# Linear attention, then a GELU projection: steps 13 to 17 of the attention in batches instead of one by one

## The chip, the cores and the metric

The kernel runs on one core of a Trainium2 chip. The metric is the time of one execution in device microseconds. Every run gives one such time; the profile is of a single execution, taken by the hardware profiler. The engines of the core are named as the profile names them: PE (TensorE, matrix multiply; PEld is its weight load), DVE (VectorE), ACT (ScalarE), POOL (GpSimd) and SP (SyncE, which issues nearly all transfers).

## The reference

Two stages. The first is a linear attention with decay, over 4 batches, 8 heads, 768 positions and 64 channels. Written in blocks:

```python
for b in range(nb):                       # 12 blocks of 64 positions
    intra = einsum('bhic,bhjc->bhij', qb, kb) * Dmask      # Dmask: lam^(i-j) where i >= j
    intra = einsum('bhij,bhjd->bhid', intra, vb)
    inter = einsum('bhid,bhde->bhie', qb * lam_pow, kv_state)
    out[:, :, sl] = intra + inter
    kv_state = lam_block * kv_state + einsum('bhsd,bhse->bhde', kb * rev_pow, vb)
```

The second takes its output as 3072 tokens of 512 channels:

```python
h = x @ w_in                              # 512 -> 2048
g = gelu_tanh(h)
out = g @ w_out                           # 2048 -> 512, float32
```

## The kernel before

**Steps.** The attention is cut into 24 steps. A step is 256 positions of one batch and four of the eight heads, so steps 2b and 2b+1 are the two halves of the heads for "super-block" b. Batches have three super-blocks each. One step goes through these pieces, named by their functions and by the tiles they write:

- `load_step(s)` (L70): three transfers of 256 KB issued by SP: q, k and v in float32.
- `prep_qk(s)`: the cast of q with its decay on DVE (L271), the cast of k on ACT (L276), both into one tile `qk`; from step 9 on, a transposing transfer issued by SP (L280) that writes `qkT`. The pool of `qkT` has four buffers, so the transpose of step n waits until step n-4 has read its own for the last time.
- `prep_v(s)`: v with the inverse decay on POOL (L258), and then the loads of step s+3.
- `scores(n)` (L327): 16 small matmuls on 64x64 quarters of PE, into two PSUM banks S.
- `causal(n)` (L337): DVE masks the two banks into the f16 tile PT, 128x512 each.
- `products(n, s)` (L362, L376, L385): into two banks OK, the products k.v of step n (16 small matmuls, 8 where a batch ends), PT.v of the step before (16 small ones), and state.q of the step before (two or four full-size ones).
- `x_out` (L462): ACT copies the output of a step into xT, the input of the second stage.
- `update(n, 0)` and `update(n, 1)`: the state t on DVE (L478 or L481) and its two-head form u on POOL (L488). u is what the step's state.q products read.

`R(n, s)` is scores, products, masks and the first update; `U(n)` is the second update. `burst(ns, ss)` does the same for several steps at once: all scores, then all PT.v into banks O (L411), all k.v into banks K (L425), all state.q (L436), and only then the masks. A burst of two steps takes four S, two O and two K banks, which are all eight banks of PSUM.

**The second stage** runs in groups of super-blocks: group 3 is super-blocks 4 and 5 (steps 8 to 11), group 4 is 6 and 7 (steps 12 to 15), group 5 is 8 and 9. `queue_group(g)` is called when the last step of a group has its output; it appends the group's pieces to a list, `filler`, and `fill(n)` takes the next n of them. For groups 3 and 4 there are 16 pieces of four matmuls 128x512 (Hps, L529), each with a GELU on ACT (L533) that empties the bank, and then 14 products of eight matmuls 128x256 (MX, MW and MY, L606), which use a scheme of seven products for eight. That scheme needs four sums of GELU outputs, `sum_g`, on DVE (gs, L576), each in two halves; `behind(k, ...)` attaches sums to the k-th piece, so that they are put on DVE's queue after it. `sum_win` (L151) forms sums of w_in on DVE, which are first read by the pieces of group 5 (L698).

**Order.** It is written out by hand: every engine works through its instructions in the order in which the program records them, and waits at the first whose inputs or buffer are not there. Steps 8 to 17 are taken one by one, in a loop over the table FILL: `fill`, `prep(n+2)`, `fill`, `R(n, n-1)`, `fill`, `U(n)`, `fill`, and a sum of w_in. Steps 18 to 23 are taken in bursts of two.

Of the kernel before, what the change touches and what calls it, by code (L numbers as in the profile page):

```python
# [9 lines left out]
FP16 = mybir.dt.float16  # L10
AF = mybir.ActivationFunctionType
ALU = mybir.AluOpType
# [3 lines left out]
def kernel(  # L16
# [10 lines left out]
    nc = tc.nc  # L27
    pin = tc.keep_in_program_order
    P = 128
    B, H, S, D = q.shape  # L30
    SB = 256
    NSB = S // SB
    HH = H // 2
# [12 lines left out]
    a16p = ctx.enter_context(tc.tile_pool(name="a16", bufs=5))  # L46
# [11 lines left out]
    ld32 = {}  # L58
# [85 lines left out]
    def sum_win(m, j, eng):  # L144

        if not wi_sum:
            wi_sum.extend(wst.tile([P, 2, 2, DFF // 2], FP16, tag=f"w{2 + i}", name=f"ws{i}")
                          for i in range(2))
        a, op, b = I_SUMS[m]
        cs, fs = slice(0, 2), slice(512 * j, 512 * j + 512)  # L150
        pin(eng.tensor_tensor(w_in_block(m, cs, fs), w_in_block(a, cs, fs),  # L151
                              w_in_block(b, cs, fs), op))
# [17 lines left out]
    def load_ahead(s):  # L170
        if s < NSTEP:
            load_step(s)
# [40 lines left out]
    dv = const.tile([P, H, 2], FP32)  # L213
# [31 lines left out]
    def prep(s):  # L245
        prep_qk(s)
        prep_v(s)

    def wide(t):
        return t.rearrange("p j h d -> p h j d")  # L250

    def decay(t, s):
        hs = halves[s % 2]
        return t[:, hs, :].unsqueeze(3).to_broadcast([P, HH, 2, D])

    def prep_v(s):
        tv = a16p.tile([P, 2, HH, D], FP16, tag="v16", name=f"v16_{s}")
        pin(nc.gpsimd.tensor_tensor(wide(tv[:]), ld32[s][2][:], decay(dv, s), ALU.mult))  # L258
        a16[s] = a16[s] + (tv,)
        if s >= 6:  # L260
            if s + 3 == FIRST_DMA_T + 1:
                load_step(s + 3, "qk")
            else:
                load_ahead(s + 3)

    def prep_qk(s):
        q32, k32, _ = ld32[s]
        tqk = a16p.tile([P, 2, 2, HH, D], FP16, tag="qk16", name=f"qk16_{s}")
        tq, tk = tqk[:, 0], tqk[:, 1]
        q_eng = nc.gpsimd if s == 3 else nc.vector  # L270
        pin(q_eng.tensor_tensor(wide(tq), q32[:], decay(dq, s), ALU.mult))  # L271
        if s == 0:
            inverse(halves[0])
            odd(halves[1])
            inverse(halves[1])
        pin(nc.scalar.activation(out=wide(tk), in_=k32[:], func=AF.Copy))  # L276
        a16[s] = (tq, tk)
        if s >= FIRST_DMA_T:
            o = qkp.tile([P, 2, 2, 2, P], FP16, tag="qkT", name=f"qkT_{s}")
            pin(nc.sync.dma_start_transpose(out=o[:].rearrange("p a j h t -> p (a j h) t"),  # L280
                                            in_=tqk[:].rearrange("p a j h d -> p (a j h d)")))
            qkT[s] = o
            if s == FIRST_DMA_T:
                load_step(s + 1, "v")
# [107 lines left out]
    def burst(ns, ss, *mix):  # L392


        for n in ns:
            scores(n)
        O = [ps_M.tile([P, 2, 2, P], FP32, tag="M", name=f"O{c}") for c in range(2)]
        seen = set()

        def start(kind, c, hl):  # L400
            new = (kind, c, hl) not in seen
            seen.add((kind, c, hl))
            return new

        qTs = [qkT.pop(s) for s in ss]
        for i, s in enumerate(ss):
            PT, tv = PTs.pop(s), a16.pop(s)[2]
            for hp in range(2):
                for jk in range(2):
                    for c, hl in TILES:  # L410
                        pin(nc.tensor.matmul(  # L411
                            O[c][half64(hl), i, hp, :], tv[half64(c), jk, 2 * hp + hl, :],
                            PT[half64(c), hl, hp, jk, :], start=start("O", c, hl), stop=False,
                            skip_group_check=True))
        if ns:
            K = [ps_M.tile([P, 2, P], FP32, tag="M", name=f"K{c}") for c in range(2)]
        for i, n in enumerate(ns):
            _, tk, tv = a16[n]
            last = (n // 2) % NSB == NSB - 1
            for jk in range(2):  # L420
                for hp in range(2):
                    for c, hl in TILES:
                        if c == 1 and last:
                            continue
                        pin(nc.tensor.matmul(  # L425
                            K[c][half64(hl), i, hp * D : hp * D + D],
                            tk[half64(c), jk, 2 * hp + hl, :], tv[half64(c), jk, 2 * hp + hl, :],
                            start=start("K", c, hl), stop=(jk == 1), skip_group_check=True))
            Kps[n] = [t[:, i] for t in K]
        for i, s in enumerate(ss):  # L430
            for c in range(2):
                if c == 0 and (s // 2) % NSB == 0:
                    continue
                u = us.pop((s, 0) if c else (s - 2, 1))
                for hp in range(2):
                    pin(nc.tensor.matmul(O[c][:, i, hp, :], u[:, hp].rearrange("p l d -> p (l d)"),  # L436
                                         qTs[i][:, 0, :, hp, half64(c)], start=False, stop=True,
                                         skip_group_check=True))
        for n in ns:
            causal(n)  # L440
        for i, s in enumerate(ss):
            x_out(s, [t[:, i].rearrange("p h t -> p (h t)") for t in O])
        sbg = ss[-1] // 2
        g, i = group_of[sbg]
        if i == len(groups[g]) - 1:
            queue_group(g, *mix)
        for n in ns:
            update(n, 0)
# [63 lines left out]
    def queue_group(g, lead=0, per_set=0):  # L512
# [69 lines left out]
        def product(m, p, part=None):  # L582
# [42 lines left out]
            def store(T, ps=slice(0, NP), es=slice(0, 2)):  # L625
                r = row0 + T * HN
                rows = out[r : r + HN, :].rearrange("(p q) (e d) -> q p e d", q=P, e=2)
                whole = g == 3 or (g, T) == (4, 0)
                for i in [ps] if whole else [slice(i, i + 1) for i in range(ps.start, ps.stop)]:
                    pin(nc.sync.dma_start(out=rows[:, i, es], in_=out_tile(T)[:, i, es, :]))  # L630

# [180 lines left out]
        def behind(k, i0, i1, ms):  # L812

            piece = filler[at + k]

            def both():
                piece()
                sum_g(i0, i1, ms)

            filler[at + k] = both  # L820
# [21 lines left out]
        if per == 2:  # L842
            behind(5, 0, 4, (1, 2))
            behind(6, 0, 4, (4, 3))
            behind(7, 4, 8, (1,))
            behind(8, 4, 8, (2,))
            behind(9, 4, 8, (4,))
            behind(10, 4, 8, (3,))
        else:
            behind(9, 0, 4, (1, 2, 4, 3))  # L850
            w = 2 if g + 1 in SEVEN else 1
            for k, m in zip((0, 3, 7, 11) if w == 2 else (0, 1, 2, 4), (1, 2, 4, 3)):
                behind(n1 + k, 4, 8, (m,))

    def fill(n):
        for _ in range(min(n, len(filler))):
            filler.pop(0)()

    def R(n, s, ahead=None):

        if n is not None:
            scores(n)
        if ahead:
            ahead()
        products(n, s)
        if n is not None:
            causal(n)
        if s is not None and s % 2 == 1:
            g, i = group_of[s // 2]
            if i == len(groups[g]) - 1 and g > 0:  # L870
                queue_group(g)
        if n is not None:
            update(n, 0)

    def U(n):
        update(n, 1)
# [63 lines left out]
    for m in W_SUMS:  # L940
# [29 lines left out]
    prep_v(9)  # L970
    fill(2)

    FILL = {8: (0, 2, 1, 2), 9: (2, 2, 1, 2), 10: (0, 1, 1, 3), 11: (0, 2, 1, 2), 12: (0, 2, 1, 3),
            13: (0, 2, 1, 3), 14: (0, 3, 1, 3), 15: (0, 2, 1, 3), 16: (0, 2, 1, 3), 17: (0, 3, 1, 3)}
    for n, (a, b, c, d) in FILL.items():
        stage_t(n)
        fill(a)
        prep_qk(n + 2) if n == 8 else prep(n + 2)
        fill(b)
        R(n, n - 1)  # L980
        fill(c)
        U(n)
        if n == 8:
            prep_v(n + 2)
        if n == 17:
            prep_qk(20)
            fill(1)
            prep_qk(21)
            fill(1)
            prep_v(20)  # L990
            prep_v(21)
            fill(1)
        else:
            fill(d)
        if 8 < n < 17:
            sum_win((n - 7) // 2, (n - 1) % 2, nc.vector)

    burst((18, 19), (17,))
    fill(2)
    U(18)  # L1000
    U(19)
# [47 lines left out]
```

## Time and profile before

| | |
|---|---|
| median of 7 runs | 200.19 us (199.78 to 202.28) |
| the profiled execution | 199.67 us, of which the span from first to last instruction is 197.9 us |
| PE busy | 192.6 us, 97% of the span |
| DVE, ACT, POOL busy | 151.8, 123.1, 73.2 us |
| granted TensorE clock | 1.000 |
| scores of step 13 / of the burst of 18 and 19 start | 86.80 / 117.74 us |

Times inside the execution are microseconds from the start of the span. In the timeline a row is `start, duration, engine, line, operation, out<-in, tile, shape, count`, and what stands in brackets is idle time before it and what ended it. The ends of matmuls are modelled; their starts can be trusted, so the cost of a stretch of PE is read from one start to another.

### The profile page before, as it was taken

The page shows a single profiled execution, that of the slowest core. Times are in us where ns is not written, and L with a number is a line of the kernel's source. Part 1 is how long each engine was busy: PE and PEld are TensorE (multiplying, and loading weights), DVE is VectorE, ACT ScalarE, POOL GpSimd, SP SyncE. Part 2 cuts the span into 40 slices and gives each one's busy share as a digit, 9 for nine tenths or more (in the row PEclk, how much of TensorE's full clock was granted, in tenths as well). Part 3 has the DMA queues.
Part 4 walks back from the last instruction along what each step waited for, and adds up shares of the span by engine and source line. Part 5 has one row for each costly group of instructions (what it writes and reads, how often), then busy time and mean ns, then how long its engine had stood idle before and what let it go on. Part 6 is the DMA issues. An engine that isn't in the chain of part 4 may idle for free.

```text
span 197.9 us, 5938 instructions
## 1 busy us (share of the span) xinstructions
PE 192.6 (97%) x2439; PEld 140.2 (71%) x2439; DVE 151.8 (77%) x296; ACT 123.1 (62%) x251; POOL 73.2 (37%) x85
## 2 busy tenths in 40 slices
PE   8979999999999999999999999999999999999993
PEld 2556544456888888754588754578888888888882
DVE  4797623689999989949898378998778997588620
ACT  3673878466793674577735486854668836778221
POOL 6594123456457643435533465056002030002000
PEclk9999999999999999999999999999999999999999
DMA  6999999999999999999854999530211300030205
GB/s 173 291 325 387 385 386 386 297 290 303 322 265 264 220 299 228 208 318 193 226 144 111 265 230 230 145 56 0 53 45 64 107 7 0 0 108 2 106 3 212
DMA packets 61706, 37.86 MB, mean 191 GB/s; under 512 B 17520, under 2 KB 54640, under 8 KB 61680
## 3 DMA queue, kind: packets, MB, share of 16 engines
q1 hardware_dynamic: 61136, 37.23, 72.9%
q8 instruction: 19, 0.31, 0.7%
q10 hardware_dynamic: 544, 0.26, 0.5%
q14 instruction: 7, 0.06, 0.1%
HBM read 27.26 MB, written 6.29 MB: 170 GB/s over the span
## 4 chain that ended last, share of the span: by engine, by line
PE 88%; SPq 4%; DMA 4%; ACT 1%; issue 1%
PE Hps L529 24%; PE MX L606 17%; PE MY L606 9%; PE HX L698 7%; PE O2ps L544 7%; PE MW L606 4%; DMA wi<-in_moe_w_in_dram 4%; SPq L70 4%; PE HY L698 4%; PE S L327 3%; PE Hps L789 3%; PE OK L385 2%; PE HW L698 2%; PE OK L376 2%; PE Tps L298 1%; PE O L436 1%
## 5 line engine op out<-in xcount | busy, mean ns | idle before, releaser
L529 PE MATMUL Hps<-xT,w_in 128*128 128x512 f16 (+1 forms) x288 | 51.0, 332 | 0.0
L488 POOL TENSOR_TENSOR u<-t,lumask 128x256 f16<-128x256 f32 x40 | 29.5, 749 | 49.2 <-DVE t L481 33.7
L529 PEld LDWEIGHTS <-w_in 128*128 128x128 f16 x288 | 27.8, 98 | 18.8
L533 ACT ACTIVATE gT<-Hps 128x512 f16<-128x512 f32 x56 | 33.1, 597 | 10.7 <-PE Hps L529 10.1
L337 DVE TENSOR_TENSOR PT<-S,mask 128x512 f16<-128x512 f32 x48 | 30.5, 681 | 7.5 <-PE S L327 7.3
L606 PEld LDWEIGHTS <-gs 128*128 128x128 f16 x320 | 31.2, 98 | 3.6
L258 POOL TENSOR_TENSOR v<-v,dv 128x512 f16<-128x512 f32 x24 | 29.7, 1240 | 7.6 <-DMA v<-in_v_dram 6.8
L606 PEld LDWEIGHTS <-gT 128*128 128x128 f16 x240 | 23.2, 98 | 3.5 <-ACT gT L533 0.5
L606 PE MATMUL MX<-w_sum,gs 128*128 128x256 f16 x160 | 21.4, 273 | 0.0
L271 DVE TENSOR_TENSOR qk<-q,dq 128x512 f16<-128x512 f32 x23 | 19.3, 842 | 0.8 <-DMA q<-in_q_dram 0.8
L576 DVE TENSOR_TENSOR gs<-gT 128x1024 f16<-128x1024 f16 (+1 forms) x24 | 18.4, 772 | 1.6 <-ACT gT L533 1.6
L651 POOL TENSOR_TENSOR o<-u,q 128x512 f32<-128x512 f32 (+1 forms) x5 | 5.3, 1054 | 37.4 <-ACT u L623 37.4
L276 ACT ACTIVATE qk<-k 128x512 f16<-128x512 f32 x24 | 15.0, 626 | 6.4 <-DMA k<-in_k_dram 6.3
L462 ACT ACTIVATE xT<-OK 128x256 f16<-128x256 f32 x34 | 13.0, 455 | 6.1 <-PE OK L385 5.8
L544 PE MATMUL O2ps<-w_out,gT 128*128 128x512 f16 x64 | 14.6, 379 | 0.0
L698 PEld LDWEIGHTS <-ws 128*128 128x128 f16 x128 | 12.5, 97 | 1.8
L623 ACT ACTIVATE u<-MX 128x256 f32<-128x256 f32 x18 | 6.9, 384 | 10.1 <-PE MX L606 10.1
L481 DVE SCALAR_TENSOR_TENSOR t<-t,lamu,OK 128x64 f32<-128x64 f32 x48 | 11.0, 273 | 1.4 <-issue 0.5
L327 PEld LDWEIGHTS <-qkT 64*64 64x64 f16 x384 | 6.1, 106 | 7.2 <-issue 3.6
L544 PEld LDWEIGHTS <-gT 128*128 128x128 f16 x64 | 6.1, 98 | 6.6
L606 PE MATMUL MY<-w_out,gs 128*128 128x256 f16 x80 | 10.7, 273 | 0.0
L606 PE MATMUL MX<-w_sum,gT 128*128 128x256 f16 x80 | 10.4, 273 | 0.0
(95 smaller groups left out, 313.3 us busy)
## 6 DMA issues: line engine op xcount, KB each, us to landing
q<-in_q_dram SPq DMA_DIRECT2D x24, 256.0 KB, 5.0
k<-in_k_dram SPq DMA_DIRECT2D x24, 256.0 KB, 5.2
v<-in_v_dram SPq DMA_DIRECT2D x23, 256.0 KB, 5.4
out_dram<-o SPq DMA_DIRECT2D x17, 256.0 KB, 3.9
wo<-in_moe_w_out_dram SPq DMA_DIRECT2D x4, 1024.0 KB, 9.5
wi<-in_moe_w_in_dram SPq DMA_DIRECT2D x4, 512.0 KB, 8.0
wi<-in_moe_w_in_dram SPq DMA_DIRECT2D x2, 1024.0 KB, 12.7
out_dram<-o SPq DMA_DIRECT2D x3, 512.0 KB, 5.7
```

The costliest lines, as they stand in the source:

```text
L258: pin(nc.gpsimd.tensor_tensor(wide(tv[:]), ld32[s][2][:], decay(dv, s), ALU.mult))
L271: pin(q_eng.tensor_tensor(wide(tq), q32[:], decay(dq, s), ALU.mult))
L276: pin(nc.scalar.activation(out=wide(tk), in_=k32[:], func=AF.Copy))
L337: pin(nc.vector.tensor_tensor(t[:, hl].rearrange("p b c d -> p b (c d)"), Sps[:].rearrange("p b c d -> p b (c d)"), mask[:].unsqueeze(1).t ...
L462: pin(nc.scalar.activation(out=d, in_=o, func=AF.Copy))
L488: pin(nc.gpsimd.tensor_tensor(u[:], state[half][:].unsqueeze(2).to_broadcast([P, 2, 2, D]), lumask[:, 2 * half : 2 * half + 2, :].unsqueez ...
L529: pin(nc.tensor.matmul(by_block(Hps[:, i, :]), w_in16[:, c, f * P : (f + 1) * P], x(c), start=(c == 0), stop=(c == NC - 1)))
L533: pin(nc.scalar.activation(out=dst, in_=Hps[:], func=AF.Gelu_apprx_tanh))
L544: pin(nc.tensor.matmul(O2[tau][0][:], gT[:, f % HF, f // HF, tau * P : (tau + 1) * P], w_out16[:, f, :], start=(n == 0), stop=(n == NF - 1)))
L576: pin(nc.vector.tensor_tensor(g_rows(m, i), g_rows(a, i), g_rows(b, i), op))
L606: pin(nc.tensor.matmul(dst, lhsT, rhs, start=(opens and i == 0), stop=(closes and i == HF - 1), skip_group_check=True))
L698: pin(nc.tensor.matmul(dst[:, i, :], w_in_block(a, slice(c, c + 1), slice(f * P, f * P + P))[:, 0], x_block(b, slice(c, c + 1))[:, 0], sta ...
```

## The change

Steps 13 to 17 leave the loop. They are taken as a burst of 13 and 14, a burst of 15 and 16, and step 17 alone; the burst of 18 and 19 now also carries the outputs of 16 and 17, not of 17 alone. `prep_qk` is split into the casts (`cast_qk`) and the transpose (`transpose_dma`), and `prep_v` into the scaling (`scale_v`) and the loads. The casts and the scaled v of 15 and 16 come ahead of the first batch, the transpose of 16 and the loads of 18 and 19 behind it. Of group 3's sums of activations, two of the first halves are attached to piece 12, behind the second batch, instead of piece 9. Four sums of w_in move behind step 17. One store of group 4 is issued in two halves.

```diff
     def prep_qk(s):
+        cast_qk(s)
+        transpose_dma(s)
+
+    def cast_qk(s):
...
         a16[s] = (tq, tk)
+        whole_qk[s] = tqk
+
+    whole_qk = {}
+
+    def transpose_dma(s):
+        tqk = whole_qk.pop(s)
         if s >= FIRST_DMA_T:
...
-        if i == len(groups[g]) - 1:
+        if ss[-1] % 2 == 1 and i == len(groups[g]) - 1:
             queue_group(g, *mix)
...
-                whole = g == 3 or (g, T) == (4, 0)
+                whole = g == 3
...
-            behind(9, 0, 4, (1, 2, 4, 3))
+            behind(9, 0, 4, (1, 2) if g == 3 else (1, 2, 4, 3))
+            if g == 3:
+                behind(12, 0, 4, (4, 3))
...
-    FILL = {8: (0, 2, 1, 2), 9: (2, 2, 1, 2), 10: (0, 1, 1, 3), 11: (0, 2, 1, 2), 12: (0, 2, 1, 3),
-            13: (0, 2, 1, 3), 14: (0, 3, 1, 3), 15: (0, 2, 1, 3), 16: (0, 2, 1, 3), 17: (0, 3, 1, 3)}
+    FILL = {8: (0, 2, 1, 2), 9: (2, 2, 1, 2), 10: (0, 1, 1, 3), 11: (0, 2, 1, 2), 12: (0, 2, 1, 3)}
...
-        if n == 17:
-            prep_qk(20)
-            fill(1)
-            prep_qk(21)
-            fill(1)
-            prep_v(20)
-            prep_v(21)
-            fill(1)
-        else:
-            fill(d)
-        if 8 < n < 17:
+        if n == 12:
+            prep_qk(15)
+            scale_v(15)
+        fill(d)
+        if n > 8:
             sum_win((n - 7) // 2, (n - 1) % 2, nc.vector)
 
-    burst((18, 19), (17,))
+    cast_qk(16)
+    scale_v(16)
+    fill(2)
+    burst((13, 14), (12,))
+    transpose_dma(16)
+    fill(1)
+    U(13)
+    U(14)
+    load_ahead(18)
+    load_ahead(19)
+    fill(6)
+    burst((15, 16), (13, 14))
+    fill(1)
+    U(15)
+    U(16)
+    prep(17)
+    fill(8)
+    prep(18)
+    R(17, 15)
+    fill(1)
+    U(17)
+    fill(1)
+    sum_win(3, 0, nc.vector)
+    fill(2)
+    prep(19)
+    sum_win(3, 1, nc.vector)
+    fill(2)
+    sum_win(4, 0, nc.vector)
+    fill(2)
+    sum_win(4, 1, nc.vector)
+    fill(2)
+    prep_qk(20)
+    fill(1)
+    prep_qk(21)
+    prep_v(20)
+    fill(3)
+
+    burst((18, 19), (16, 17))
+    prep_v(21)
     fill(2)
```

More of the change, by code (lines that the diff above doesn't have):

```diff
@@ L256, in prep_v @@
     def prep_v(s):
-        tv = a16p.tile([P, 2, HH, D], FP16, tag="v16", name=f"v16_{s}")
-        pin(nc.gpsimd.tensor_tensor(wide(tv[:]), ld32[s][2][:], decay(dv, s), ALU.mult))
-        a16[s] = a16[s] + (tv,)
+        scale_v(s)
         if s >= 6:
@@ L264, in prep_v, with scale_v @@
                 load_ahead(s + 3)
+    def scale_v(s):
+        tv = a16p.tile([P, 2, HH, D], FP16, tag="v16", name=f"v16_{s}")
+        pin(nc.gpsimd.tensor_tensor(wide(tv[:]), ld32[s][2][:], decay(dv, s), ALU.mult))
+        a16[s] = a16[s] + (tv,)
     def prep_qk(s):
+        cast_qk(s)
+        transpose_dma(s)
+    def cast_qk(s):
         q32, k32, _ = ld32[s]
```

## The prediction

> **What bounds the kernel now.** I read the head of the page first, then PE's timeline around steps 13 to 21, then the timelines of DVE and SP there and the answer on the tile qkT.
>
> ```profile
> span 197.9 us, 5938 instructions
> PE 192.6 (97%) x2439; PEld 140.2 (71%) x2439; DVE 151.8 (77%) x296; ACT 123.1 (62%) x251; POOL 73.2 (37%) x85
> PE 88%; SPq 4%; DMA 4%; ACT 1%; issue 1%
> ```
>
> PE is the bound: 97% busy, 88% of the chain that ended last. A change in this stretch is worth what it takes from PE's own work, less any hole that it opens there.
>
> PE's timeline: step 13 alone, the burst of 18 and 19 with one output, the burst of 20 and 21 with two.
>
> ```profile
> 86.80 0.42 PE L327 MATMUL S<-qkT 64*64 64x128 f16 x16
> 87.04 0.29 PE L362 MATMUL OK<-v,qk 64*64 64x64 f16 x16
> 87.17 0.40 PE L376 MATMUL OK<-PT,v 64*64 64x128 f16 x16
> 87.50 0.28 PE L385 MATMUL OK<-qkT,u 128*128 128x128 f16 x2
> 87.62 6.21 PE L529 MATMUL Hps<-xT,w_in 128*128 128x512 f16 x28
> ...
> 117.74 0.64 PE L327 MATMUL S<-qkT 64*64 64x128 f16 x32
> 118.21 0.39 PE L411 MATMUL O<-PT,v 64*64 64x128 f16 x16
> 118.44 0.50 PE L425 MATMUL K<-v,qk 64*64 64x64 f16 x32
> 118.87 0.40 PE L436 MATMUL O<-qkT,u 128*128 128x128 f16 x4
> 119.10 7.07 PE L529 MATMUL Hps<-xT,w_in 128*128 128x512 f16 x32
> 126.10 0.64 PE L327 MATMUL S<-qkT 64*64 64x128 f16 x32
> 126.57 0.62 PE L411 MATMUL O<-PT,v 64*64 64x128 f16 x32
> 127.02 0.45 PE L425 MATMUL K<-v,qk 64*64 64x64 f16 x32
> 127.40 0.40 PE L436 MATMUL O<-qkT,u 128*128 128x128 f16 x4
> 127.64 2.75 PE L529 MATMUL Hps<-xT,w_in 128*128 128x512 f16 x12
> ```
>
> Read the starts. PE runs on without a hole here; a step costs from its first S to the next large matmul: 0.82 us alone, 1.36 and 1.54 in a burst. Before its first S there is about 0.1 more: 28 Hps take 6.13 us to the next S (93.75), 16 take 3.55 (114.19 to 117.74), so one takes 0.215 and 0.1 is left over.
>
> The transposes on SP, and the casts of q on DVE:
>
> ```profile
> 86.32 2.34 SPq L280 DMA_TRANSPOSE qkT<-qk  x1
> 92.41 1.24 SPq L280 DMA_TRANSPOSE qkT<-qk  x1
> DMA to landing us min/median/max: 3.1/5.5/6.6
> 97.38 1.10 DVE L271 TENSOR_TENSOR qk<-q,dq 128x512 f16<-128x512 f32 x1
> 110.22 0.69 DVE L271 TENSOR_TENSOR qk<-q,dq 128x512 f16<-128x512 f32 x1
> ```
>
> A transpose lands 3.1 to 6.6 us after its issue; asked one by one, those issued at 92.41, 99.37 and 106.71 took 3.3, 3.1 and 3.2, the one at 86.32, with three loads and two stores still under way, 5.8. A cast of q takes 0.69 us with POOL idle and 1.10 with POOL at work.
>
> **The gain on PE.** The same matmuls are issued, in fewer groups. Before: single steps 0.82 (13), 0.83 (14) and 0.93 each (15 to 17, two more state.q), the burst 1.36, and six entries of 0.1: 6.4 us. After, pieces priced by the rows above (state.q 0.06 each from 118.87 to 119.10; eight k.v 0.10 from 127.02 to 127.40): burst of 13 and 14 with output 12, 1.36 less two state.q, 1.25; burst of 15 and 16, 1.54 with eight k.v less and two state.q more, 1.56; step 17, 0.93; burst of 18 and 19 with two outputs, 1.54 and four state.q more, 1.77; four entries 0.4. Sum 5.9. Gain 0.5 us, and no more: PE has no hole in this stretch that could close. [...]
>
> **Walk for holes.** I follow the new order with durations of these rows; nothing changes before step 13 starts at 86.80.
>
> *Burst of 13 and 14.* The transpose of 14 was issued at 80.98 and landed after 4.4 us, at 85.4. On DVE the cast of 16 is added ahead of the masks (0.7 to 1.1 us), into an idle time of 2.43 us; its q was loaded from 77.57 with 5.3 us to landing. On ACT the cast of k of 15 goes into the idle 0.48 us before the first GELU and that of 16 takes 15's old place, so the last K bank comes free at 87.5 as before, just when K wants it: 0 to 0.1 us. On POOL the scaled v of 16 is done by 87, the first u is due at 90. Free, all of it. Next Hps at 86.80 + 1.25 = 88.05.
>
> *Burst of 15 and 16.* Seven Hps pieces of 0.865 and an entry: 94.2. The transpose of 15 goes at about 85.5, behind two stores (84.51, 0.92), that of 16 only when step 12's qkT is read, 88.1. The nearest pair, issued at 116.4 and 119.4, landed after 6.4 and 5.8: 16 at 93.9, needed at 94.4. Hidden by 0.5; at 6.6 us a hole of 0.3. DVE: four masks, a copy, six state updates, two sums, done by 93.9 at the longest rows; masks of 15 at 94.66 (0.46 after S, as at 86.80 and 87.26).
>
> *Step 17* is the tight place. Its prep was a whole step ahead; now its cast of q stands on DVE behind the masks of 15 and 16 and the two sums moved there. Masks 2.41 us (126.56 to 128.97), four updates 0.76, two sums 1.2 (0.61 each, POOL idle) to 1.8 (122.52 to 124.32, POOL at work), two updates 0.38, the cast 0.69 to 1.10: done at 100.1 to 101.1. POOL has four items of its own there (three u of 15 and 16, the scaled v of 17), so I take the later half: 100.9. Both loads (18 and 19, issued from 90 to 94) should have landed by 100, since landing took 3.7 to 6.5 us, so the transpose takes 3.2: 104.1. PE meanwhile: 94.2 + 1.56 + four Hps 3.46 + five products of 0.874 + 0.1 = 103.7. Hole 0.4 to 0.5; bounds 0 (cast at 100.1, 3.1) and 4.0 us (101.1, 6.6). I take 0.5. Queued behind that wait on PE are the remaining products; all of PE shifts.
>
> [...] The row at 97.38 shows 1.10 while POOL was busy from 97.00 on, so the measured value is taken.
>
> *Burst of 18 and 19.* 104.2 + 0.93 + nine products 7.87 + five Hps 4.33 + 0.1 = 117.4, by when casts and transposes of 18 and 19 (cast by 106 and 109) are long there. The four sums of w_in (four of 0.7 to 1.1) lie on DVE between 107 and 113, first read at 135. The scaled v of 21 goes behind it, needed with the next K, 7 us on. Next Hps at 119.2 (119.10 before).
>
> *Transposes of 20 and 21* both wait for this burst, since 16 and 17 are read there; before, only 21 did (119.4). Issued at about 119.2 and 120.5; with no load ahead of them both should be there by 125 (21 by 126.3 at 5.8 us); needed at 126.2 and 126.5. Hidden by 1 us or so; at 6.6 us a hole of 0.6.
>
> *The rest.* The split store: one more issue of 0.44 us on SP at 137, with nobody behind it that PE waits for. From 126 on the order is the old one.
>
> **Sum.** -0.5 on PE, +0.5 in the hole before step 17, 0 elsewhere: the profiled execution's 199.67 stays. That execution stands 0.5 below the median of 200.19; on the median's scale I forecast 200.2. A measurement tells about 0.5%, 1 us, from no change.
>
> **Rivals.**
> - *No hole.* The two sums run fast and the cast at 0.69: 103.2 to 103.5 against 103.7. For it: POOL's u of 15 may end before the cast starts. Time 200.2 - 0.5 = 199.7.
> - *Slower: the transpose of 17 lands late.* The one at 127.76 took 4.7 us with hardly any other transfer under way, so quiet queues are no guarantee, and loads of 18 and 19 that are still under way would make it 5.8 to 6.6. Hole 101 + 4.7 - 103.7 = 2.0 up to 4.0, less 0.5: +1.5 to +3.5, 201.7 to 203.7. It decides once the landing takes over 4.2 us. Against it: the three nearest took 3.1 to 3.3.
> - *Transposes of 20 and 21 late.* A hole of 0.6 to 1.5 if both run at 6.4 us one behind the other: 200.8 to 201.7. Against it: the two queued at 116.4 had three loads and a store ahead of them, the new ones nothing.
> - *The batches save nothing on PE* (the small matmuls run slower against a K bank that comes free late): 200.2 + 0.5 = 200.7. Against it: the existing bursts.
>
> **Numbers.** Forecast 0.48, no hole 0.20, 17 late 0.20, 20 and 21 late 0.07, no saving 0.05. Most of the late cases and a little of the forecast's own upper end are over 1 us slower: 0.26. Faster by over 1 us is reached only if the no-hole case meets a low draw of runs (they spread from 199.78 to 202.28): 0.08. Within: 0.66. The range goes from no hole with 0.3 of scatter, 199.4, to a landing of 5.1 us, 202.1.
>
> **What would show it.** Right: after the change S of step 13 still starts near 86.8, the next Hps 1.25 later, the burst of 15 and 16 near 94.2; PE idles by 0.2 to 0.9 us before the scores of 17 at about 104, waiting for a transposing transfer; the burst of 18 and 19 takes 1.77 and ends within 0.4 of 119.2. Wrong: a wait of PE or PEld before the scores of 16, 20 or 21; a hole at 17 of over 1 us (a late landing) or none; a burst that takes as long as two single steps; or DVE behind PE in the products after step 17, so that sums (gs) rather than transposes hold PE.

## The result, and the profile after

The changed kernel takes 203.28 us in the median of 12 runs (201.59 to 204.86); the kernel before, run beside it, takes 199.89 (31 runs). The ratio is 1.0132, with a 95% interval of 1.0108 to 1.0156. So the change costs 1.3%, and the time lies above the range of the forecast, 199.4 to 202.1.

The runs of the changed kernel fall into two groups, which a median hides: 201.59 to 201.90 at a granted clock of 1.000 (four runs) and 203.21 to 203.40 at 0.992 (seven). Executions far from all others of their kernel are left out of such counts: 204.86 us here, 1103.68 and 500.77 us in two of the experiments. The profiled execution is of the second group: 203.21 us, span 201.3, 3.4 more than before.

The head of the page of the changed kernel, its row of granted clocks, and the queue table's line for the fetching of instructions (packets, MB, share of the 16 DMA engines):

```profile
span 201.3 us, 5933 instructions
PE 193.7 (96%) x2439; PEld 141.5 (70%) x2439; DVE 155.0 (77%) x296; ACT 122.7 (61%) x251; POOL 74.4 (37%) x85
PEclk9999999999999999999996999999999999999999
PE 86%; DMA 6%; SPq 4%; ACT 1%; issue 1%
...
q8 instruction: 19, 0.31, 0.7%
```

PE still has the same 2439 matmuls and is still the bound, but DMA has gone from 4% to 6% of the chain that ended last, and one slice of the clock row, of 5 us and just past 105 us, shows a 6. Both point at the same place. PE's timeline there:

```profile
86.75 0.64 PE L340 MATMUL S<-qkT 64*64 64x128 f16 x32
...
88.00 6.21 PE L542 MATMUL Hps<-xT,w_in 128*128 128x512 f16 x28
94.14 0.64 PE L340 MATMUL S<-qkT 64*64 64x128 f16 x32
...
95.75 3.62 PE L542 MATMUL Hps<-xT,w_in 128*128 128x512 f16 x16
...
102.70 1.04 PE L619 MATMUL MY<-w_sum,gs 128*128 128x256 f16 x8
105.97 0.64 PE L340 MATMUL S<-qkT 64*64 64x128 f16 x16 [2.24 <-DMA qkT<-qk]
...
120.70 0.64 PE L340 MATMUL S<-qkT 64*64 64x128 f16 x32
...
122.43 7.07 PE L542 MATMUL Hps<-xT,w_in 128*128 128x512 f16 x32
```

The starts up to 102.70 are those of the walk in the prediction, to 0.1 us. Then PE stands still for 2.24 us before the scores of step 17, and what ends the wait is the transposing transfer. No matmul of step 17 can start without it.

Two microseconds are not all of it. From the scores of step 13 to the Hps behind the burst of 18 and 19 the profiled execution takes 122.43 - 86.75 = 35.68 us, before it took 119.10 - 86.80 = 32.30: 3.38 more. The hole explains 2.24 of that. The windows of the profiled execution (busy microseconds of PE, PEld, DVE, ACT and POOL with their instructions, the granted clock, the mean busy share of the DMA engines, and GB/s) show the rest; the last four are cut closely around the two moments at which the clock changes:

```profile
104.00:106.00 2.00, 0.03 (x4) 0.03 (x4) 2.00 (x4) 0.00 (x0) 0.14 (x1) 0.97 1.01 286
106.00:108.00 2.00, 2.00 (x46) 1.72 (x47) 1.77 (x3) 0.39 (x2) 0.00 (x0) 0.50 0.40 104
108.00:110.00 2.00, 2.00 (x15) 1.55 (x13) 1.82 (x4) 0.81 (x3) 1.18 (x2) 0.67 0.89 177
110.00:112.00 2.00, 2.00 (x21) 1.80 (x19) 1.72 (x2) 1.29 (x4) 1.17 (x1) 1.00 1.02 295
...
105.50:105.89 0.39, 0.00 (x0) 0.00 (x0) 0.39 (x2) 0.00 (x0) 0.00 (x0) 1.00 0.87 232
105.90:106.30 0.40, 0.33 (x14) 0.33 (x17) 0.40 (x1) 0.00 (x0) 0.00 (x0) 0.50 0.96 265
108.90:109.30 0.40, 0.40 (x4) 0.28 (x3) 0.40 (x2) 0.00 (x0) 0.40 (x1) 0.50 0.71 145
109.32:109.70 0.38, 0.38 (x5) 0.35 (x4) 0.38 (x1) 0.14 (x1) 0.38 (x2) 1.00 0.56 85
```

After the hole the granted clock is 0.50, from 105.90 to 109.31, and then 1.00 again; the 0.67 is the mean of the window that holds its return. PE is busy all the while, but with 15 instructions in two microseconds where the next window has 21. A PE that reads as 100% busy (2.00 of 2.00 us from 106 to 108) had half its clock there (0.50): the column of the clock is the one that tells.

The transfer itself, by the chain of work that ended last and by SP's timeline:

```profile
100.91 5.02 DMA qkT<-qk
```

```profile
100.91 1.24 SPq L293 DMA_TRANSPOSE qkT<-qk  x1
102.20 0.57 SPq L70 DMA_DIRECT2D q<-in_q_dram  x1
102.82 0.55 SPq L70 DMA_DIRECT2D k<-in_k_dram  x1
103.48 0.44 SPq L70 DMA_DIRECT2D v<-in_v_dram  x1
```

It was issued when the prediction had it (100.9), and landed after 5.02 us, not 3.2. On SP's queue the three loads of step 20 follow right behind. The packets of the DMA engines add something: a packet of 16 KB of the queue that fetches instructions, 0.92 us long, starts at 103.86, when the packets of the transpose are just ending. Such a packet comes 19 times in an execution, by the line of the queue table above.

### The profile page after: what moved, and what is told of

Read it like the earlier page. It is cut to its first block, busy times and chain, and to the rows that moved or that the text cites. A ratio compares the mean times of both kernels' runs of the same rounds, so it can differ in the third digit from the quotient of the medians.

```text
span 201.3 us, 5933 instructions
## 1 busy us (share of the span) xinstructions
PE 193.7 (96%) x2439; PEld 141.5 (70%) x2439; DVE 155.0 (77%) x296; ACT 122.7 (61%) x251; POOL 74.4 (37%) x85
## 4 chain that ended last, share of the span: by engine, by line
PE 86%; DMA 6%; SPq 4%; ACT 1%; issue 1%
PE Hps L542 24%; PE MX L619 17%; PE MY L619 9%; PE HX L711 7%; PE O2ps L557 7%; DMA wi<-in_moe_w_in_dram 4%; SPq L70 4%; PE HY L711 4%; PE MW L619 3%; PE S L340 3%; PE Hps L802 3%; DMA qkT<-qk 2%; PE HW L711 2%; PE OK L398 2%; PE OK L389 1%; PE O L449 1%
## 5 line engine op out<-in xcount | busy, mean ns | idle before, releaser
L501 POOL TENSOR_TENSOR u<-t,lumask 128x256 f16<-128x256 f32 x40 | 30.1, 767 | 49.5 <-DVE t L494 31.9
L619 PEld LDWEIGHTS <-gs 128*128 128x128 f16 x320 | 31.7, 99 | 4.0
L278 DVE TENSOR_TENSOR qk<-q,dq 128x512 f16<-128x512 f32 x23 | 20.1, 879 | 0.7 <-DMA q<-in_q_dram 0.7
L475 ACT ACTIVATE xT<-OK 128x256 f16<-128x256 f32 x26 | 10.0, 456 | 10.0 <-PE OK L398 9.8
L340 PE MATMUL S<-qkT 64*64 64x128 f16 x384 | 9.3, 224 | 3.1 <-DMA qkT<-qk 2.2
L475 ACT ACTIVATE xT<-O 128x256 f16<-128x256 f32 x22 | 8.0, 459 | 5.9 <-PE O L449 5.0
L619 PE MATMUL MY<-w_sum,gs 128*128 128x256 f16 x80 | 11.1, 287 | 0.0
```

Of the source, the lines that this page charges most:

```text
L340: pin(nc.tensor.matmul(Sps[hl][half64(c), hp, jk, :], o[half64(hl), 1, jk, hp, half64(c)], o[half64(hl), 0, :, hp, half64(c)], start=True, ...
L475: pin(nc.scalar.activation(out=d, in_=o, func=AF.Copy))
L501: pin(nc.gpsimd.tensor_tensor(u[:], state[half][:].unsqueeze(2).to_broadcast([P, 2, 2, D]), lumask[:, 2 * half : 2 * half + 2, :].unsqueez ...
L619: pin(nc.tensor.matmul(dst, lhsT, rhs, start=(opens and i == 0), stop=(closes and i == HF - 1), skip_group_check=True))
```

## The experiments

Three questions were open. Was it the landing that cost the time, and what made it late: the loads behind it on the queue, the instruction packet, or an ordinary spread? Did the clock fall because PE waited for 2 us? And what is the change worth without the hole? All kernels below are the changed kernel with one edit. Ratios are to the kernel before, run on the same chip.

**Loads of step 20 moved behind the transpose of step 18.**

```diff
-    prep(17)
+    prep_qk(17)
+    scale_v(17)
     fill(8)
-    prep(18)
+    prep_qk(18)
+    scale_v(18)
+    load_ahead(20)
+    load_ahead(21)
     R(17, 15)
```

> The loads of step 20 are issued behind the transpose of step 18 instead of right behind that of step 17; nothing else changes, all work is done. In the changed kernel the transpose of 17 was issued at 100.91 and landed after 5.0 us, and PE stood still for 2.24 us. Theory 'loads': the three loads queued right behind the transpose hold up its last part; then it lands here after about 3.2 us, the hole shrinks to 0.4 and the time is about 199.9. Theory 'instruction fetch': a 16 KB packet of the instruction queue, in the trace at 103.86 us and 0.92 us long, stands on one DMA engine in front of the transpose's end; then the loads don't matter, the landing stays at about 5.0, the hole at 2.2, and the time at 201.7 to 203.3 (the two clusters of the changed kernel).

Measured: 201.62 us (201.49 to 201.69, 4 runs), ratio 1.0089 [1.0074, 1.0104], at full clock. PE's timeline of this run:

```profile
104.46 0.42 PE L340 MATMUL S<-qkT 64*64 64x128 f16 x16 [0.50 <-DMA qkT<-qk]
...
119.53 0.42 PE L340 MATMUL S<-qkT 64*64 64x128 f16 x16 [1.46 <-DMA qkT<-qk]
```

The transpose of 17 landed after 3.3 us, and the hole before step 17 is the forecast's 0.5, as the forecast had it with a landing of 3.2. But the time did not come back, because the six loads now stand in front of the transpose of step 19, which was issued at 111.82 and landed after 7.7 (112.18 and 3.1 in the changed kernel): a hole of 1.46 before the scores of 19. The hole was moved, not closed. An instruction packet was near the end of the transpose of 17 here too (103.85, 2.7 after the issue) and did no harm; the packets below show why.

**The instruction packets moved in time by small extra matmuls.** 48 matmuls of 8 columns in the warm-up, into a bank that is not used yet, so that the same fetches come at another point of the program; the loads stay.

```diff
-    def idle(n, wide=0):
+    def idle(n, wide=0, tiny=0):
...
+        dt = mybir.dt.bfloat16
+        for _ in range(tiny):
+            pin(nc.tensor.matmul(t[:, 0:8], ones[dt][:, 0:P], ones[dt][:, 0:8],
                                  start=True, stop=True))
...
-    idle(3)
+    idle(3, tiny=48)
```

> 48 extra matmuls of 8 columns stand in the warm-up before step 0 ends (about 1 us of PE at 9 us, where the loads of w_in are what is waited for), so PE reads 96 more instructions and its instruction blocks are fetched earlier by some 3 to 4 us at step 17; the computation is unchanged. Theory 'instruction fetch': the packet at 103.86 moves to about 100, before the transpose of 17 is under way; it lands after 3.2 us, the hole is about 0.4, the granted clock stays at 1.0 and the time is 199.7 to 200.3. Theory 'loads': landing 5.0, hole 2.2, 201.7 to 203.3 as in the changed kernel.

Measured: 203.02 us (200.97 to 203.59, 4 runs), ratio 1.0142 [1.0089, 1.0195]. With no instruction packet near, and the loads still behind, the transpose of 17 landed after 3.1 us and the hole is 0.34. The total says nothing about the change, because the extra matmuls disturbed the start: step 13 begins 3.2 us later (89.94), and PE stands still for 2.1 us, from 14.5 to 16.6 us, with a halved clock behind it. The profile shows nothing that it waits for there (`issue`), so the cause is not shown. PE's row and a window of this run (columns as above):

```profile
16.61 0.32 PE L393 MATMUL OK<-PT,v 64*64 64x128 f16 x2 [2.11 <-issue]
...
18.00:20.00 2.00, 2.00 (x26) 1.33 (x24) 1.02 (x2) 1.32 (x4) 0.00 (x0) 0.52 1.06 388
```

**The same with less disturbance**: 28 small matmuls at 17 us, into a bank that is overwritten afterwards.

```diff
+    dt = mybir.dt.bfloat16
+    for _ in range(28):
+        pin(nc.tensor.matmul(banks[0][0][:, 0:8], ones[dt][:, 0:P], ones[dt][:, 0:8],
+                             start=True, stop=True, skip_group_check=True))
     products(3, None, banks)
```

> The changed kernel with 28 extra matmuls of 8 columns at 17 us, where PE waits for a load of w_in, so that the instruction packet which stands at 103.86 us in the changed kernel comes about 3 us earlier relative to step 17; everything else stays, the loads of 20 right behind the transpose of 17 included. If the late landing needs the instruction packet, the transpose of 17 lands after 3.1 to 3.3 us, the hole is 0.3 to 0.5, and the time is 199.9 to 200.5 (up to 0.5 for the extra matmuls). If the loads behind it are enough, landing 5.0, hole 2.2, 201.7 to 203.5.

Measured: 200.29 us (199.82 to 201.13, 10 runs), ratio 1.0018 [0.9999, 1.0036]: 3 us less than the changed kernel's median, with 28 matmuls more. The instruction packet started 0.78 us before the issue of the transpose; the loads stood behind it as before. The landing was 3.1 us, and PE's timeline has:

```profile
104.55 0.42 PE L340 MATMUL S<-qkT 64*64 64x128 f16 x16 [0.34 <-DMA qkT<-qk]
```

The lowest clock of its ten runs is 0.998. Of the 20 runs of the kernel before beside it, 19 lie at 1.000 and one at 0.991, with 200.71 us: a lower clock is not quite unknown to the kernel before.

**The cast of step 17 ahead of the two sums.** All of `prep(17)` moves up: the casts, the transpose, the scaled v and the loads.

```diff
     burst((15, 16), (13, 14))
+    prep(17)
     fill(1)
     U(15)
     U(16)
-    prep(17)
     fill(8)
```

> The cast and the transpose of step 17 are put right behind the second batch, ahead of the two sums and of the second updates. Cast done at about 98.5 instead of 100.8, transpose issued there. Under either theory of the late landing it is there by 103.6 (98.6 + 5.0) while PE wants it at 103.7: no hole or one under 0.2, clock 1.0, PE's saving of 0.5 is left and the time is 199.4 (before 199.9). If the hole has another cause (PE waits for sums or banks), the time stays above 201.

Measured: **199.55 us** (199.40 to 199.69, 10 runs), ratio 0.9982 [0.9972, 0.9991]: 1.8% less than the change and slightly better than the kernel before. The timelines of DVE and then PE in this run; the transpose was issued at 99.24:

```profile
98.09 1.01 DVE L278 TENSOR_TENSOR qk<-q,dq 128x512 f16<-128x512 f32 x1
```

```profile
87.07 0.64 PE L340 MATMUL S<-qkT 64*64 64x128 f16 x32
...
103.02 1.04 PE L619 MATMUL MY<-w_sum,gs 128*128 128x256 f16 x8
103.99 0.42 PE L340 MATMUL S<-qkT 64*64 64x128 f16 x16
112.78 4.48 PE L542 MATMUL Hps<-xT,w_in 128*128 128x512 f16 x20
...
118.92 7.07 PE L542 MATMUL Hps<-xT,w_in 128*128 128x512 f16 x32
```

The cast is done at 99.10 in place of 100.77, the transpose goes 1.67 us earlier (2.0 us, counted from the scores of step 15, which start at 94.46 here) and lands after 3.1 us, and the row of the scores of 17, at 103.99, has no wait. From step 13 to the Hps behind the burst of 18 and 19 it takes 118.92 - 87.07 = 31.85 us, where before it took 32.30: the batches are worth 0.45 us on PE. This also sorts the 35.68 us of the changed kernel: 31.85, the hole of 2.24, and 1.53 for the halved clock are 35.62. The last term can be read directly. From the scores of 17 to the next Hps, the same matmuls take 116.29 - 105.97 = 10.32 us in the changed kernel and 112.78 - 103.99 = 8.79 here.

**The two sums of activations put back behind piece 9**, the batches kept.

```diff
-            behind(9, 0, 4, (1, 2) if g == 3 else (1, 2, 4, 3))
-            if g == 3:
-                behind(12, 0, 4, (4, 3))
+            behind(9, 0, 4, (1, 2, 4, 3))
```

> The changed kernel with all four first halves of group 3's sums attached to piece 9 again, ahead of the second batch; batches and everything else as changed. Theory 'the two moved sums delay the cast of 17': DVE reaches that cast 1.8 us earlier (the two sums took 97.77 to 99.71), the transpose goes at about 99.1 and is there by 102.3 to 104.1, the hole is 0 to 0.4, and the time is 199.5 to 199.9; the masks of 15 come 0.3 us later, which nobody waits for. If instead the sums ahead of the batch hold up the masks and with them the banks, PE stops after the second batch and the time stays near 200.5 or above.

Measured: 199.62 us (199.44 to 200.48, 10 runs), ratio 0.9996 [0.9984, 1.0007]. The cast of 17 starts at 99.03, 4.01 us after the scores of step 15 (95.02) in place of 5.95 in the changed kernel; its transpose, issued at 99.86, lands after 3.1, and there is no hole; the stretch takes 31.85 us here too. The masks of step 15 still start 0.46 us after the scores, so the sums in their old place do not hold the masks up:

```profile
95.48 2.48 DVE L350 TENSOR_TENSOR PT<-S,mask 128x512 f16<-128x512 f32 x4
...
99.03 0.69 DVE L278 TENSOR_TENSOR qk<-q,dq 128x512 f16<-128x512 f32 x1
```

**More products ahead of step 17**, so that PE reaches its scores later. First two pieces more (the two single pieces around `U(17)` go to the front), then one.

```diff
     prep(18)
+    fill(2)
     R(17, 15)
-    fill(1)
     U(17)
-    fill(1)
```

> Two product pieces (1.75 us) are taken ahead of step 17 instead of behind it. The transpose lands at 105.9 as before, PE arrives at 105.4 instead of 103.7: hole 0.5 instead of 2.24. If the halved clock after the hole (0.50 from 106 to 109.5 in the changed kernel) comes from the length of the hole, it stays at 1.0 here and the time is 199.9 + 1.8 - 1.75 = 199.9. If any hole or the small matmuls of the step alone bring it about, the clock still drops and the time is about 201.5.

Measured: 200.08 us (199.79 to 200.35, 10 runs), ratio 1.0014 [1.0005, 1.0023]. The landing is as late as in the changed kernel, 5.1 us, but only 0.53 of it is left as a hole, and the clock does not fall behind it (0.997 to 1.000 in the ten runs).

```diff
     prep(18)
+    fill(1)
     R(17, 15)
-    fill(1)
     U(17)
     fill(1)
```

> One product piece (0.87 us) is taken ahead of step 17 instead of behind it. Landing 5.0 as in the changed kernel, hole 1.4 instead of 2.24. If the clock is halved only after a hole of about 2 us or more, it stays at 1.0 in every run and the time is 200.8 in one cluster. If the clock reacts to a hole of any length at this place, there are again two clusters, at 200.8 and 202.4.

Measured: 200.95 us (200.91 to 201.08, 4 runs), ratio 1.0055 [1.0041, 1.0070]. Landing 5.0, hole 1.33, full clock in all runs (0.997 to 1.000), one group. So the late landing alone did not lower the clock.

**Fewer products ahead of step 17**: one, two and three pieces taken from the `fill(8)` and given to the `fill` behind `R(17, 15)`. These make the hole longer.

```diff
-    fill(8)
+    fill(7)
     prep(18)
     R(17, 15)
-    fill(1)
+    fill(2)
     U(17)
```

> One product piece less ahead of step 17: hole 3.1 instead of 2.24. If the length of the hole decides on the clock, nearly every run has the halved clock for 3 to 4 us afterwards: one cluster at 199.9 - 0.5 + 3.1 + 1.6 = 204.1. If the drop is a matter of chance in each run, there are two clusters at 202.5 and 204.1 in about the shares of the changed kernel (5 to 7).

Measured: 200.96 us (200.73 to 201.87, 4 runs), ratio 1.0064 [1.0040, 1.0087]. The expectation fell, and by its own cause: with the order changed, the instruction packet no longer met the transpose, which landed after 3.1 us. The hole is 1.23 us, not 3.1, and the clock stays at 1.000. The slowest run, the profiled one, had another 0.8 us of waiting for a GELU at 61 us.

```diff
-    fill(8)
+    fill(6)
     prep(18)
     R(17, 15)
-    fill(1)
+    fill(3)
     U(17)
```

> Two product pieces (1.75 us) are taken behind step 17 instead of ahead of it: PE wants its scores at about 102.0. With one piece less the instruction packet no longer met the transpose, which landed after 3.1 us; the same here: landing at about 104.1, hole 2.1, so a hole of the changed kernel's length without its late landing. If the length of the hole decides on the clock, two clusters as in the changed kernel, 201.5 (clock 1.0) and 203.1 (clock 0.99). If the drop in the changed kernel came with the late transfer and not with the length, one cluster at 201.5.

Measured: 203.42 us (five runs: 201.81 and 203.16 to 203.44), ratio 1.0176 [1.0159, 1.0193]. The transpose landed after 3.1 us. PE's row in the profiled execution, which is the one at 201.81:

```profile
104.38 0.42 PE L340 MATMUL S<-qkT 64*64 64x128 f16 x16 [2.09 <-DMA qkT<-qk]
```

A hole of the changed kernel's length, made without a late transfer, brings back the two groups: one run at a clock of 0.998, four at 0.990 to 0.992, 1.6 us apart. So a hole of this length lowered the clock without a late transfer. That it doesn't in every run, the profiled one among those, is taken up in the last section.

```diff
-    fill(8)
+    fill(5)
     prep(18)
     R(17, 15)
-    fill(1)
+    fill(4)
     U(17)
```

> Three product pieces (2.6 us) are taken behind step 17: hole 3.0 at a landing of 3.1. If a hole of over 2 us is what halves the clock and 2.2 is just at the edge, every run has the drop: one cluster at 204.0, clock 0.99. If the drop is a matter of chance: two clusters, 202.4 and 204.0.

Measured: 202.66 us at a clock of 1.000, 204.28 and 204.40 at 0.989 and 0.992; ratio 1.0194 [1.0150, 1.0238]. The profile of this kernel is of the execution of 500.77 us, so its hole of about 3 us is worked out from 202.66 - 199.55, not seen. Even there one run in three kept its full clock.

**All runs together.** With 199.55, the time of the version without a hole, the time at full clock is that plus the hole. (The kernels ran on different chips; the median of the kernel before was 199.82 to 199.89 on all of them.)

| kernel | landing of 17 | hole at 17 | 199.55 + hole | measured at full clock | runs at a clock of 0.990 to 0.992, and their time |
|---|---|---|---|---|---|
| two sums back | 3.1 | 0 | 199.6 | 199.62 | none |
| two pieces more | 5.1 | 0.53 | 200.1 | 200.08 | none |
| one piece less | 3.1 | 1.23 | 200.8 | 200.73 to 200.96, and 201.87 with the wait at 61 us | none |
| one piece more | 5.0 | 1.33 | 200.9 | 200.95 | none |
| loads later | 3.3 | 0.50, and 1.46 at 19 | 201.5 | 201.62 | none |
| two pieces less | 3.1 | 2.09 | 201.6 | 201.81 | 4 of 5, 203.16 to 203.44 |
| the changed kernel | 5.0 | 2.24 | 201.8 | 201.59 to 201.90 | 7 of 11, 203.21 to 203.40 |

The two kernels with small matmuls are left out, since these cost time themselves, and so is three pieces less, whose hole was not seen.

And the landings, from the packets of the DMA engines (times relative to the issue of the transpose of step 17):

```
kernel             instruction packet starts    three loads right behind    landing
changed kernel            +2.95                        yes                   5.0
two pieces more           +2.98                        yes                   5.1
one piece more            +2.93                        yes                   5.0
loads later               +2.7                         no                    3.3
28 small matmuls          -0.78                        yes                   3.1
48 small matmuls          none near                    yes                   3.1
cast first                none near                    yes                   3.1
two sums back             none near                    yes                   3.1
one piece less            none near                    yes                   3.1
two pieces less           none near                    yes                   3.1
```

That the packet is a cause is shown by its moves: shifted away by 28 or 48 small matmuls, with the loads still behind, it leaves a landing of 3.1. It does not need the loads behind it, as the transpose of step 22 shows in the same traces (issued at 127.76 in the kernel before, at 131.08 in the changed one), which has no transfer behind it. In nine kernels an instruction packet starts 2.3 to 2.9 us after its issue, and it lands after 4.5 to 4.9 us. In the two kernels with small matmuls the packet starts 0.13 and 0.36 us after the issue, and the landings are 3.1 and 3.5.

The packets also show what is held back. In the traces a transpose is 1024 packets of 256 bytes and 32 of four bytes; the four-byte ones come at its end:

```
transpose                  four-byte packets                     instruction packet    landing
17, changed kernel         30 by 103.54, the next at 104.54      103.86 to 104.78      5.0
17, two pieces more        30 by 103.66, the next at 104.71      104.02 to 104.94      5.1
17, one piece more         30 by 103.78, the next at 104.73      104.06 to 105.01      5.0
17, loads later            all 32 by 103.85                      103.85 to 104.77      3.3
22, changed kernel         30 by 133.67, two at 134.86, 134.87   133.93 to 134.88      4.8
22, kernel before          30 by 130.34, two at 131.74           130.28 to 131.20      4.7
```

In each late case only 30 of the 32 are out in time. At step 22, with no loads, the last two come with the end of the instruction packet or after it; at step 17 they can't be told from the four-byte packets of the loads, but none at all comes for a microsecond. In the run with later loads all 32 were out just as the packet started, so that it had nothing to hold back: the early landing there is not the work of the loads. Which of the DMA engines a packet used is not on record, so whether the two and the instruction packet shared one is not shown.

## Why the prediction was wrong

**Right: the gain on PE.** Forecast 0.5, measured 0.45 (32.30 against 31.85). The burst of 13 and 14 took 88.00 - 86.75 = 1.25, as forecast; that of 15 and 16 took 1.61 against 1.56; that of 18 and 19 took 1.73 against 1.77.

**Right: the walk.** Next Hps at 88.00 (88.05), burst of 15 and 16 at 94.14 (94.2), transpose of 17 issued at 100.91 (cast done at 100.9), no wait before the scores of 16, 20 and 21. The step called the tight place was the place. The two sums and the cast were sized a little off in opposite ways: sums of 1.00 and 1.09 us against 0.6 to 0.9 apiece, a cast of 0.68 against 0.69 to 1.10. The issue on time is so far luck. The prediction took the 1.10 us of the row at 97.38 as the longest that a cast lasts with POOL at work; but that row, and one of 1.53 us at 63.31 in the same profile, both end 0.55 us after the POOL instruction behind which they started (last section). The cast of 17 started 0.16 us before POOL's u and took 0.68.

**Wrong: "so the transpose takes 3.2: 104.1."** It took 5.02. The other terms were right, so the hole became 0.5 + 1.8 = 2.3; 2.24 measured. The inference stood on the three nearest transposes before, which had landed after 3.1 to 3.3 with loads behind them but no instruction packet between issue and landing. The forecast asked only whether transfers issued earlier would still be under way. It didn't look at the line of the instruction queue, 0.7% of the engines' time, because it is nothing in the mean; one packet at one moment was what mattered. The row at 127.76, which took 4.7 in quiet queues, was seen and cited, and left without a cause; it had an instruction packet at its end.

So the rival "the transpose of 17 lands late" happened, with a price that fits: 200.2 - 0.5 + 2.24 = 201.9, the slow end of the four runs at full clock (the kernel before, at 199.89 rather than 200.2, makes it 201.6). Its chance of 0.20 and its threshold (4.2 us of landing) were on record; of the two sources given for it, loads of 18 and 19 still under way and a spread seen at 127.76 without a cause, it was the second.

**Wrong by a missing term: the clock.** Every case priced a hole at its own length. A hole of 2.24 us cost 3.8 in seven of eleven runs: its own length and 1.53 for matmuls at half clock. That is what puts the median at 203.28 instead of near 201.8.

**What in the change did it.** Not the batches: with the two sums back at their place, or with the cast of 17 ahead of them, the batches give 199.62 and 199.55. The two sums behind the second batch put the cast of q off by 1.94 us (5.95 instead of 4.01 after the scores of 15). This uses up the slack ahead of step 17 (0.5 us short even with a landing of 3.3, as the run with later loads shows) and moves the transpose to where an instruction packet meets its end. The first was foreseen; the second was not.

## What to carry to other kernels

Where a change shifts a transfer to the edge of its slack, price it with the slowest landing in the trace and not with its nearest neighbours, unless the cause of the slow ones is known and excluded; the few packets that fetch instructions are one such cause, and edits as small as one piece of products moved them here (one piece more: packet at +2.93, landing 5.0; one piece less: none near, landing 3.1). A hole of 2.24 us in the matrix engine cost 3.8 in seven of eleven runs, and two short ones were cheaper than one long one here: 0.50 and 1.46 us left all four runs at full clock (201.62 us), 2.09 us in one piece did so in one run of five (median 203.42). When a batch saves work on the bound engine, put the cast and the transfer of the tight step ahead of work that nobody waits for yet: that order alone made the difference between 203.28 and 199.55 us here.

## What the runs showed of the hardware

**The clock after a hole.** Holes of 0.3 to 1.5 us, in 32 runs of five kernels, left the granted clock at 0.997 or more. At 2.1 to 2.24 us the mean clock of most runs is 0.990 to 0.992: 7 of 11 (the changed kernel), 4 of 5 (two pieces less) and 3 of 4 (48 small matmuls, with its hole at 14.5 us). (Each hole is read in the one profiled execution of its kernel.) In the two of these runs that have a profile the clock is 0.50 for 3.41 us (105.90 to 109.31 in the changed kernel, 16.50 to 19.92 with 48 small matmuls). The drop costs 1.5 to 1.6: 1.53 in the changed kernel, 1.6 between the groups of two pieces less.

Why not in every run? The traces keep the moments at which the clock changes. In all eleven (three pieces less apart) each stretch at one clock, from the first at full clock to the drop when PE has no more work, is a whole multiple of 3.413 us: 1, 3, 27, 29, 53, 56 and 57 times. So in these traces the clock changes only at the edges of a grid of 3.413 us, and the grid does not lie at the same place in every execution: it has an edge at 105.90 in the changed kernel and at 103.54 in two pieces less. In the changed kernel the step of the grid that ended at 105.90 held 2.16 us in which PE stood still; with 48 small matmuls the step that ended at 16.50 held 2.00. Both were followed by half clock. In the profiled execution of two pieces less, which kept its clock, the edge at 103.54 cuts the hole of 2.09 us into 1.25 and 0.84. The most in any step without a drop behind it is 1.46 us (loads later). So in these traces half clock follows the steps with 2.00 and 2.16 us of standing still, and none with 1.46 or less. That the place of the edge decides for holes of 2.1 to 2.24 us, and so makes the two groups of times, is the author's reading of these three profiles; no other run of the three kernels has one. The run of the kernel before at 0.991 has no profile, so its cause stays open.

**The instruction packet.** The packet that met the transpose took 0.92 us; the 19 of the execution took 0.92 to 1.46. Where one started 2.3 to 3.0 us after the issue of the transpose of step 17 or 22, which otherwise took 3.1 to 3.5 us, and before its last four-byte packets were out, the landing came after 4.5 to 5.1 us, with loads behind it or without. Where it fell into the middle of a transpose, 1.08 and 1.17 us after its issue, the landings were 4.2 (step 18 with 48 small matmuls) and 4.0 us (two pieces less, at 105.74).

**The cast and POOL.** The prediction read 0.69 us for a cast of q with POOL idle and 1.10 with POOL at work. The rows show that the cast's end followed the end of POOL's instruction, if POOL began first. The first pair is from the kernel before, the other two from the changed kernel:

```profile
97.00 0.93 POOL L488 TENSOR_TENSOR u<-t,lumask 128x256 f16<-128x256 f32 x1 [0.22 <-DMA q<-in_q_dram]
97.38 1.10 DVE L271 TENSOR_TENSOR qk<-q,dq 128x512 f16<-128x512 f32 x1
...
84.20 1.49 POOL L266 TENSOR_TENSOR v<-v,dv 128x512 f16<-128x512 f32 x1
84.71 1.52 DVE L278 TENSOR_TENSOR qk<-q,dq 128x512 f16<-128x512 f32 x1
...
100.09 0.68 DVE L278 TENSOR_TENSOR qk<-q,dq 128x512 f16<-128x512 f32 x1
100.25 1.00 POOL L501 TENSOR_TENSOR u<-t,lumask 128x256 f16<-128x256 f32 x1 [1.01 <-DVE t L494]
```

In the first two pairs the cast starts while POOL is at work and ends 0.55 us after POOL does (98.48 after 97.93, 86.23 after 85.69). So do, to 0.01 us, all but three of the 72 casts that started behind a POOL instruction after 55 us, in eleven traces; the longest took 1.75 us. In the third pair the cast of 17 started first: it took 0.68, as with POOL idle (0.68 at 105.81), and it was POOL's u that took 1.00 in place of 0.61 (at 77.52). With the sums back the cast (99.03, 0.69 us) came 0.03 us ahead of the second u.
